# A state-space scan and a SwiGLU feed-forward on one core: smaller pieces of converted weights, and a last block that is stored in quarters and eighths

## The chip, the cores and the metric

The kernel runs on one core of a Trainium2 chip, in one launch. The metric is the device time of that core in microseconds. A core has TensorE (PE in the profile; PEld is its weight load), VectorE (DVE), ScalarE (ACT), GpSimd (POOL), SyncE (SP), which here issues nearly all DMAs, and 16 DMA engines.

## The reference

Two stages. The first is a Mamba-2 scan over x (4 batches, 8 heads, 768 tokens, 32 channels) with decays `a` and state matrices B and C (16 wide); its result, as 3072 tokens of 256 channels, is the input of the second, a gated feed-forward. Shortened:

```python
# scan, in chunks (the kernel takes 128 tokens as a chunk)
L = exp(cum[i] - cum[j]) * causal
y = ((C @ B.T) * L) @ x  +  (C @ state) * exp(cum)
state = exp(sum(la)) * state + sum_j B_j x_j * exp(cum[-1] - cum[j])
# feed-forward: x is (3072, 256), d_ff is 1536
xn = x / sqrt(mean(x * x) + 1e-6) * rms_g
g, val = xn @ w_gate, xn @ w_val
out = (g / (1 + exp(-g)) * val) @ w_out
```

w_gate, w_val and w_out come as 64-bit floating point, all else in 32 bits; the kernel makes 32-bit numbers of the weights on the chip.

## The kernel before

The 3072 tokens are worked on in six blocks of 512. While block n goes through the feed-forward, the scan makes the input of block n + 1, so that PE's products of both are interleaved. Blocks 1 to 5 take the products two by two in Strassen's way with seven products instead of eight (`product_gv`, steps P.k.j with k = 1 to 7 and j = 0 to 5 for 256 columns of d_ff; `product_o`, steps O.k.j). Sums of weights that these need are made by VectorE (`combine_w`, step cw; `combine_wo`, step two), sums of inputs too (`combine_x`, step tx; s, s2, s3, s4 for the hidden values). The partial results are taken out of PSUM by ScalarE (take), added by VectorE (C), go through SiLU on ScalarE (silu) and are multiplied on VectorE (hid). Block 0 takes the first columns with plain products (early.0, early.1, gate.2 to gate.5), the others in Strassen's way (there silu and hid are called silug and hidg), and its products with w_out are plain (o.0 to o.11).

The order of all this is written out by hand or by a planner: a string of steps for block 0, one for block 1, one for blocks 2 to 4 and one for block 5. The kernel runs through the string, and each engine executes its instructions in the order in which the steps issue them. A step that waits therefore holds up what comes after it on its engine.

Conversion of the weights is part of block 0. `fetch` issues the DMAs of a piece on SP's queue, as raw 32-bit words. `power(k)` (step pow) makes the power of two from the top 16 bits with three ScalarE instructions (lines 165, 166, 168), `mantissa(k)` (step man) makes the mantissa with two VectorE instructions (lines 175, 177), `weight(k)` (step wt) multiplies both (line 185) and issues the next fetch. Pieces before: two of 128 columns of both w_gate and w_val (512 elements a partition), five of 256 columns of both, three of w_out (1024 elements a partition each). The mantissa is made in the raw buffer itself; three large raw buffers exist.

Other steps that the prediction speaks of: spread fetches rows of sums of logarithms by a broadcast DMA, sub and ex (line 407) make decays of them, after which GpSimd masks them (line 408); load fetches B, C and x of a pair of chunks; rowout stores the sums of logarithms; turn, T, Tt, g, L, L1, A, S, y, sq, yt belong to the scan; ms, mc, mt, rs, rb, xn to the normalisation.

In block 5 the scan is over, and only the feed-forward runs. Its last product with w_out is k = 3, which adds onto product 5 in one PSUM bank, for two groups t of 128 tokens and 128 channels (a block is two groups t by two halves a of 128 tokens); `total_o` adds the taken partial results (Oadd, line 844) and `put_half` stores half a of the block's tokens, 256 KB, in one DMA (out, line 849).

Of the kernel before, what the change touches and what calls it, by code (L numbers as in the profile page):

```python
# [20 lines left out]
def kernel(  # L21
# [33 lines left out]
    nc = tc.nc  # L55
# [72 lines left out]
    pieces = [("gv", c, 128) for c in (0, 128)] + [("gv", c, 256) for c in range(256, DF, 256)]  # L128
    pieces += [("o", c, 4) for c in range(0, NF, 4)]
    fetched = []  # L130

    def fetch(k=1):
        for _ in range(min(k, len(pieces))):
            n, c, w = pieces.pop(0)
            if w == 128:
                r = ffn.tile([P, 8 * w], I32, tag="h", name="wr", bufs=NF // 2)
            else:
                r = raw.tile([P, 8 * 256], I32, tag="wr", name="wr", bufs=3)
            if n == "o":
                nc.sync.dma_start(out=r.rearrange("p (o m) -> p o m", o=w),  # L140
                                  in_=wsrc[n][:, c:c + w])
                dst = wo[:, c:c + w].rearrange("p o m -> p (o m)")
            else:
                both = r.rearrange("p (n t f) -> p n t f", n=2, t=2)
                for k, name in enumerate("gv"):
                    nc.sync.dma_start(out=both[:, k], in_=wsrc[name][:, :, 2 * c:2 * (c + w)])
                dst = wgv[:, :, :, c:c + w]
            w32 = r.rearrange("p (f w) -> p f w", w=2)
            fetched.append((r.bitcast(I16).rearrange("p (f w) -> p f w", w=4)[:, :, 3],
                            w32[:, :, 0], w32[:, :, 1], dst, w32.shape[1]))  # L150
# [10 lines left out]
    def power(k):  # L161
        words16, lo, hi, dst, n = fetched[k]
        e = cvt.tile([P, n], FP32, tag="e", name="e", bufs=2)
        k16, b16 = e.bitcast(I16)[:, n:2 * n], e.bitcast(I16)[:, 0:n]
        nc.scalar.activation(out=k16, in_=words16, func=AF.Relu, scale=1.0 / 16, bias=kinks[:, 0:1])  # L165
        nc.scalar.activation(out=e, in_=k16, func=AF.Prelu, scale=-1.0, bias=kinks[:, 1:2],  # L166
                             alpha=2.0 ** -20)
        nc.scalar.activation(out=b16, in_=e, func=AF.Prelu, scale=-2.0 ** 27, bias=kinks[:, 2:3],
                             alpha=2.0 ** -20)
        parts[k] = b16.bitcast(BF16)  # L170


    def mantissa(k):
        words16, lo, hi, dst, n = fetched[k]
        nc.vector.tensor_scalar(out=hi, in0=hi, scalar1=0xFFFFF, scalar2=0x100000,
                                op0=ALU.bitwise_and, op1=ALU.bitwise_or)
        nc.vector.scalar_tensor_tensor(out=lo.bitcast(FP32), in0=lo.bitcast(U32),
                                       scalar=2.0 ** -32, in1=hi, op0=ALU.mult, op1=ALU.add)

    def weight(k):  # L180
        words16, lo, hi, dst, n = fetched[k]
        f, e = lo.bitcast(FP32), parts.pop(k)
        if len(dst.shape) > 2:
            f, e = [v.rearrange("p (n t f) -> p n t f", n=2, t=2) for v in (f, e)]
        nc.vector.scalar_tensor_tensor(out=dst, in0=f, scalar=2.0 ** -20, in1=e,  # L185
                                       op0=ALU.mult, op1=ALU.mult)
        if k > 1:
            fetch()


    start = ffn.tile([P, 8, P], FP32, tag="ob", name="start", bufs=1)
    warm = start[:, 0].bitcast(BF16)
# [8 lines left out]
    fetch(1)  # L201
    gcol = const.tile([P, 2], FP32, name="gcol")
    nc.sync.dma_start(out=gcol, in_=moe_rms_g.rearrange("(t p) -> p t", p=P))
    fetch(2)
    load(2)
    load_x(2)
    fetch(2)
# [6 lines left out]
    ones = start[:, 5]  # L214
    nc.vector.memset(ones, 1.0)
    zeros = start[:, 1]
    nc.vector.memset(zeros, 0.0)
    upto = start[:, 2]
    nc.gpsimd.affine_select(out=upto, in_=ones, pattern=[[1, P]], compare_op=ALU.is_ge,
                            fill=0.0, base=0, channel_multiplier=-1)  # L220
    never = start[:, 3]
    nc.gpsimd.affine_select(out=never, in_=zeros, pattern=[[1, P]], compare_op=ALU.is_ge,
                            fill=-2.0 ** 100, base=0, channel_multiplier=-1)
    after = start[:, 4]
# [72 lines left out]
    mids = start[:, 6:8]  # L297
# [396 lines left out]
    spaces = []  # L694

    def piece_for_sums(k):
        while len(spaces) <= k // 2:
            spaces.append(raw.tile([P, 2, 8 * P], FP32, tag="wr", name="sums", bufs=3))
        return spaces[k // 2][:, k % 2]

    def combine_w(j):
        if j < NF // 4:
            s = piece_for_sums(j).rearrange("p (w k m) -> p w k m", w=2, k=4)
        else:
            s = const.tile([P, 2, 4, P], FP32, name="sw%d" % j)
# [39 lines left out]
    def taken_gv(blk, k, j):  # L745
        vs[k, j] = t = cvt.tile([P, 512], FP32, tag="p", name="p", bufs=4)
# [33 lines left out]
    def combine_wo(j0):  # L780
        js = slice(j0, j0 + 2)
        two[j0 // 2] = w = piece_for_sums(3 + j0 // 2).rearrange("p (k j m) -> p k j m", k=4, j=2)
# [29 lines left out]
    def product_o(blk, k, j):  # L812
        bank_of = {1: "X", 6: "X", 7: "X", 2: 2, 4: 4, 5: 5, 3: 5}[k]
        if k in (1, 2, 4, 5) and j == 0:
            val = k in (2, 5)
            Os[bank_of] = later[val].tile([P, 512], FP32, tag="val" if val else "gate",
                                          name="o", bufs=2)
# [7 lines left out]
        for t in range(2):  # L825
            nc.tensor.matmul(out=o[:, t * P:(t + 1) * P], lhsT=lhsT[:, t], rhs=rhs,  # L826
                             start=(k in (1, 2, 4, 5) and j == 0 and t == 0), stop=True,
                             skip_group_check=True)
# [11 lines left out]
    def total_o(blk, c):  # L840
        if blk not in obs:
            obs[blk] = ffn.tile([P, 2, 2, DM], FP32, tag="ob", name="ob", bufs=1)
        a, m, v, o = {11: (0, 0, 1, 2), 22: (1, 1, 7, 5), 21: (1, 0, 7, 4), 12: (0, 1, 6, 5)}[c]
        nc.vector.tensor_tensor(out=obs[blk][:, :, a, m * P:(m + 1) * P], in0=ts[v],
                                in1=halves_of(Os[o]), op=ALU.add)

    def put_half(blk, a):
        dst = out[blk * TB:(blk + 1) * TB, :].rearrange("(t a p) m -> p t a m", t=2, a=2)
        nc.sync.dma_start(out=dst[:, :, a], in_=obs[blk][:, :, a])

# [71 lines left out]
    def by_vector(out, in_, scale):  # L922
# [39 lines left out]
        mask.0.1 r.0 d parts.0 c turn.0.0 T.0.0 Tt.0.0.0 turn.0.1 sums.0.1 turn.1.0 T.0.1  # L962
        mask.0.0 Tt.0.0.1 Tt.0.1.0 dx sums.0.0 cx Tt.0.1.1 g.0.0 exp.0.1 T.1.0 turn.1.1 Tt.1.0.0
        scale.1 mask.1.1 exp.0.0 T.1.1 Tt.1.1.0 cc scale.0 L.0.0 Tt.1.0.1 sums.1.1 g.0.1
        Tt.1.1.1 A.0 g.1.1 exp.1.1 mask.1.0 pow.0 L.0.1 S.0 last.0 g.1.0 last.1 L.1.1 Tl.0
        sums.1.0 Tl.1 A.1 exp.1.0 y.0 man.0 r.1 sq.0 S.1 pow.1 L.1.0 wt.0 y.1 yt.0 ydone.0
        parts.1 scale.2 sq.1 early.0.0 pow.2 yt.1 man.1 mask.2.0 ms.0 mc.0 wt.1 sums.2.0 row.1
        ydone.1 early.0.1 mt.0 mask.2.1 rs.0 sums.2.1 turn.2.0 rowout.1 exp.2.0 mask.3.1 man.2
        exp.2.1 rb early.1.0 rc T.2.0 xn.0 Tt.2.0.0 norm.0 sums.3.1 early.1.1 wt.2 Tt.2.0.1
        pow.3 mask.3.0 exp.3.1 man.3 turn.2.1 row.0 T.2.1 Tt.2.1.0 sums.3.0 rowout.0 scale.3  # L970
        exp.3.0 Tt.2.1.1 pow.4 wt.3 gate.2 norm.1 gg.2 silu.0 pow.5 gate.3 load.4 A.2 man.4
        L.2.0 silu.3 L1.2.2 hid.0 wt.4 spread.8 S.2 silu.2 gate.4 hid.3 L1.2.3 switch.0 silu.1
        turn.3.1 hid.2 turn.3.0 T.3.0 silu.4 P.1.3 T.3.1 Tt.3.0.0 man.5 Tt.3.1.0 hid.4 take.1.3
        Tt.3.0.1 gate.5 table Tt.3.1.1 tx.0 silu.5 cw.3 wt.5 hid.5 cw.4 pow.6 y.2 P.1.4 A.3
        P.6.3 yt.2 take.6.3 gg.3 sq.2 S.3 man.6 P.7.3 take.1.4 L1.3.2 take.7.3 L.3.0 pow.7
        ydone.2 switch.1 L1.3.3 P.2.3 P.6.4 C.11.3 y.3 P.5.3 take.6.4 wt.6 P.4.3 tok man.7
        silug.21.3 P.2.4 yt.3 silug.11.3 hidg.21.3 P.7.4 sq.3 P.1.5 ms.1 C.22.3 hidg.11.3
        take.1.5 P.3.3 C.11.4 cw.5 wt.7 tokout take.7.4 C.12.3 P.5.4 silug.11.4 spread.9 ydone.3
        P.6.5 P.2.5 C.22.4 silug.22.3 silug.12.3 hidg.11.4 take.6.5 C.11.5 P.3.4 hid.1 mc.1
        pow.8 P.7.5 silug.22.4 sub.9 P.4.4 take.7.5 man.8 P.5.5 mt.1 hidg.12.3 hidg.22.3 wt.8  # L980
        o.0 rs.1 o.1 silug.21.4 o.2 C.22.5 spread.10 C.12.4 sub.8 o.3 P.3.5 pow.9 hidg.22.4
        silug.12.4 man.9 sub.10 spread.11 o.4 hidg.21.4 P.4.5 wt.9 scale.4 hidg.12.4 rb
        silug.22.5 C.12.5 ex.10 o.5 load.5 silug.11.5 sub.11 o.6 silug.21.5 xn.1 o.7 hidg.11.5
        hidg.22.5 ex.11 o.8 cw.0 o.9 ex.9 silug.12.5 hidg.21.5 hidg.12.5 o.10 cw.1 ex.8 tx.1
        o.11
# [19 lines left out]
    def of_chunk(n, fn):  # L1005
# [5 lines left out]
        "O": product_o, "Otake": taken_o, "Oadd": total_o, "out": put_half,  # L1011
        "cw": lambda blk, j: combine_w(j) if blk == 1 else None,
# [16 lines left out]
    for blk in range(1, NBLK):  # L1029
        if blk == 1:  # L1030
            order = """
                P.2.0 scale.1 P.1.1 P.1.0 P.2.1 take.1.1 turn.0.0 take.1.0 P.6.0 load.0 table
                C.11.1 P.5.1 take.6.0 P.6.1 take.6.1 P.7.0 silu.11.1 C.11.0 turn.0.1 silu.11.0
                take.7.0 T.0.0 P.7.1 P.5.0 two.0 take.7.1 P.4.0 Tt.0.0.0 C.22.1 hid.11.1
                silu.22.1 P.3.1 Tt.0.0.1 C.22.0 silu.21.0 T.0.1 silu.22.0 hid.21.0 P.4.1 P.1.2
                silu.21.1 hid.11.0 Tt.0.1.0 take.1.2 C.12.1 P.2.2 cw.2 P.3.0 spread.0 P.6.2
# [102 lines left out]
```

## Time and profile before

| | |
|---|---|
| median of 9 runs | 418.65 us (418.6 to 419.82) |
| the profiled execution | 418.61 us |
| its span, first to last instruction | 416.9 us |
| granted TensorE clock | 1.000 |
| PE busy | 410.2 us (98%), 3100 instructions |
| DVE busy | 309.1 us (74%), 635 instructions |
| ACT busy | 223.2 us (54%), 434 instructions |
| POOL busy | 41.3 us (10%), 48 instructions |
| DMA | 27.99 MB, 86516 packets |

Time outside the span (418.61 - 416.9 = 1.7 us) is that of the launch. Block 0 ends on PE at 99.0 us, block 1 at about 164.4, blocks 2 to 4 take about 64.6 us each and block 5 the last 55 us, up to the last matmul at 413.2 us. A timeline line gives start, duration (of the merged instructions from first to last), engine, line of the kernel, operation, what is written from what, shapes, how many, and in square brackets how long the engine was idle before and what ended that.

### The profile page before, as it was taken

The numbers are of one execution on the slowest core, as the hardware profiler recorded it, in microseconds if no ns is written. First come the engines' busy times: TensorE is split into PE (matmuls) and PEld (weight loads), VectorE is DVE, ScalarE is ACT, GpSimd is POOL, SyncE is SP. The second block draws the span as 40 slices with busy tenths as digits, with TensorE's granted clock in tenths as the row PEclk, the third lists the DMA queues.
The fourth block names the chain that finished last, engine by engine and source line by source line (L and its number), as shares of the span: only waits on it lengthen the run. The fifth ranks groups of instructions, "written<-read, shape, count | busy, mean of one in ns | idle before, by whom it ended". The sixth has DMA issues, their size and how long they took to land.

```text
span 416.9 us, 7846 instructions
## 1 busy us (share of the span) xinstructions
PE 410.2 (98%) x3100; PEld 343.9 (82%) x3100; DVE 309.1 (74%) x635; ACT 223.2 (54%) x434; POOL 41.3 (10%) x48
## 2 busy tenths in 40 slices
PE   8999999999999999999999999999999999999996
PEld 4675468888887899887899887889888889988996
DVE  6899899997767997566888567778667874555771
ACT  3789987987564434654418645326755421254410
POOL 3010010031000024000005100004200001000000
PEclk9999999999999999999999999999999999999999
DMA  9988846402303060505230503440100000100001
GB/s 111 228 241 209 195 152 254 49 1 61 42 2 103 22 131 0 102 2 89 63 102 20 83 2 68 85 102 2 51 2 1 2 2 0 52 1 2 0 2 50
DMA packets 86516, 27.99 MB, mean 67 GB/s; under 512 B 75952, under 2 KB 80304, under 8 KB 86480
## 3 DMA queue, kind: packets, MB, share of 16 engines
q1 hardware_dynamic: 82320, 27.24, 28.3%
q10 hardware_dynamic: 4160, 0.26, 0.7%
q8 instruction: 24, 0.39, 0.4%
q14 instruction: 12, 0.10, 0.1%
HBM read 24.22 MB, written 3.28 MB: 66 GB/s over the span
## 4 chain that ended last, share of the span: by engine, by line
PE 91%; ACT 4%; DVE 3%; issue 1%; DVEq 0%; ACTq 0%
PE gate L741 28%; PE o L826 23%; PE val L741 21%; PE o L773 5%; PE g L470 3%; PE y L552 2%; PE tp L436 2%; PE y L543 1%; PE gate L660 1%; PE A_ps L503 1%; PE e L365 1%; ACT e L166 1%; ACT e L165 1%; PE idle L268 1%; PE rb L615 1%
## 5 line engine op out<-in xcount | busy, mean ns | idle before, releaser
L753 DVE TENSOR_TENSOR c<-val,p 128x512 f32<-128x512 f32 x99 | 67.0, 687 | 42.1 <-PE val L741 32.2
L747 ACT COPY p<-gate 128x512 f32<-128x512 f32 x99 | 57.4, 585 | 64.4 <-PE gate L741 64.2
L766 DVE TENSOR_TENSOR h<-c 128x256 f32<-128x256 f32 x99 | 43.4, 459 | 11.6 <-ACT c L762 11.5
L762 ACT ACTIVATE c<-c 128x256 f32<-128x256 f32 x99 | 38.4, 416 | 13.5 <-DVE c L753 13.4
L741 PE MATMUL gate<-tx,sw 128*128 128x256 f32 x144 | 36.4, 382 | 0.0
L741 PE MATMUL gate<-xn,wgv 128*128 128x256 f32 x132 | 34.5, 389 | 0.7 <-DVE wgv L185 0.7
L838 ACT COPY v<-o 128x256 f32<-128x256 f32 x15 | 5.6, 372 | 53.3 <-PE o L826 53.3
L741 PE MATMUL val<-xn,wgv 128*128 128x256 f32 x132 | 33.9, 379 | 0.0
L741 PE MATMUL gate<-tx,wgv 128*128 128x256 f32 x132 | 33.8, 384 | 0.0
L826 PE MATMUL o<-wo,h 128*128 128x128 f32 x240 | 33.8, 275 | 0.0
L826 PE MATMUL o<-sums,h 128*128 128x128 f32 x240 | 32.7, 276 | 0.0
L571 POOL TENSOR_TENSOR sq<-sq 128x256 f32<-128x256 f32 x12 | 9.9, 824 | 225.3 <-ACT sq L570 194.9
L826 PE MATMUL o<-sums,s 128*128 128x128 f32 x240 | 31.8, 277 | 0.0
L741 PEld LDWEIGHTS gate<-tx,sw 128*128 128x128 f32 x144 | 27.0, 190 | 4.6 <-issue 0.7
L826 PEld LDWEIGHTS o<-wo,h 128*128 128x128 f32 x240 | 30.2, 192 | 0.2 <-issue 0.2
L826 PEld LDWEIGHTS o<-sums,h 128*128 128x128 f32 x240 | 29.6, 192 | 0.6 <-DVE h L766 0.5
L741 PE MATMUL gate<-tx,sums 128*128 128x256 f32 x120 | 30.0, 379 | 0.0
L826 PEld LDWEIGHTS o<-sums,s 128*128 128x128 f32 x240 | 29.1, 192 | 0.8 <-issue 0.8
L741 PEld LDWEIGHTS gate<-tx,wgv 128*128 128x128 f32 x132 | 24.6, 190 | 4.4 <-issue 1.0
L741 PEld LDWEIGHTS gate<-xn,wgv 128*128 128x128 f32 x132 | 23.5, 190 | 5.3 <-DVE h L766 1.5
L741 PEld LDWEIGHTS val<-xn,wgv 128*128 128x128 f32 x132 | 25.0, 190 | 3.4
L762 ACT ACTIVATE u<-gate 128x256 f32<-128x256 f32 x33 | 12.3, 381 | 24.3 <-PE gate L741 24.3
(165 smaller groups left out, 772.0 us busy)
## 6 DMA issues: line engine op xcount, KB each, us to landing
L<-rowd SPq DMA_DIRECT2D x16, 512.0 KB, 4.7
xr<-in_x_dram SPq DMA_DIRECT2D x24, 128.0 KB, 3.4
wr<-in_moe_w_out_dram SPq DMA_DIRECT2D x3, 1024.0 KB, 6.1
wr<-in_moe_w_gate_dram SPq DMA_DIRECT2D x5, 512.0 KB, 5.9
wr<-in_moe_w_val_dram SPq DMA_DIRECT2D x5, 512.0 KB, 6.8
out_dram<-ob SPq DMA_DIRECT2D x10, 256.0 KB, 2.2
br<-in_B_dram SPq DMA_DIRECT2D x22, 64.0 KB, 4.3
cr<-in_C_dram SPq DMA_DIRECT2D x22, 64.0 KB, 3.3
```

Of the source, the lines that this page charges most:

```text
L436: nc.tensor.transpose(out=tp[:, k], in_=src[:, i].rearrange("p h n -> p (h n)"), identity=ident)
L470: nc.tensor.matmul(out=g[:, 256 * i:256 * i + 256], lhsT=T[r, i, 0], rhs=T[r, i, 1:3].rearrange("p t m -> p (t m)"), start=(i == 0), stop= ...
L552: nc.tensor.matmul(out=y[o:o + 32, h // 4, i * P:(i + 1) * P], lhsT=s["x"][:, i, h], rhs=Ls[p][:, i, h], start=opens, stop=True, tile_posi ...
L571: nc.gpsimd.tensor_tensor(out=sqs[blk][:, tk], in0=sq2[:, 0], in1=sq2[:, 1], op=ALU.add)
L741: nc.tensor.matmul(out=dst[:, half[w]], lhsT=lhsT, rhs=rhs, start=(k in (1, 2, 5) and w == 0), stop=True, skip_group_check=True)
L747: nc.scalar.copy(out=t, in_=Xs[j])
L753: nc.vector.tensor_tensor(out=t, in0=Zs[j], in1=a, op=ALU.add)
L762: nc.scalar.activation(out=u, in_=src[:, half[0]], func=AF.Silu)
L766: nc.vector.tensor_tensor(out=hidden_tile(blk, j)[:, c // 10 - 1, c % 10 - 1], in0=u, in1=src[:, half[1]], op=ALU.mult)
L773: nc.tensor.matmul(out=o, lhsT=hs_[blk, f // 2][:, f % 2, k // 2, (k % 2) * P:(k % 2 + 1) * P], rhs=wo[:, f], start=opens, stop=(f == NF - ...
L826: nc.tensor.matmul(out=o[:, t * P:(t + 1) * P], lhsT=lhsT[:, t], rhs=rhs, start=(k in (1, 2, 4, 5) and j == 0 and t == 0), stop=True, skip ...
L838: nc.scalar.copy(out=ts[k], in_=halves_of(Os["X"]))
```

## The change

Three things change together.

- The weights are converted in pieces of half the size, each of one matrix: for w_gate and w_val two pieces each of 128 columns (256 elements a partition) and five each of 256 columns (512), for w_out six of two rows of tiles (512). So pow, man and wt number 0 to 19 instead of 0 to 9. The raw buffers are six of half the size (and four small ones); the mantissa is written to a tile of its own (`m`), so a raw buffer is free after pow and man. wt issues a fetch each time. The tiles of `taken_gv` share four buffers with the powers' (`e`). The first constants no longer share a tile with the output.
- In block 5 the last product's bank is split: product 5 and product 3 of each 128 tokens t accumulate in two banks of their own. The last product runs for t = 0, then for t = 1 (`products_of_t`, step Ot); Oadd.12 is made for each t apart; of half a = 0 the first 128 channels are stored for both t at once (128 KB, quarter.0.0), the other 128 channels for each t apart (64 KB, quarter.0.1.0 and quarter.0.1.1). Half a = 1 is stored as before.
- All four orders are new.

```diff
+    wdst = {"g": wg, "v": wv, "o": wo}
+    pieces = [(n, c, w) for c, w in [(0, 128), (128, 128)] + [(c, 256) for c in range(256, DF, 256)]
+              for n in "gv"]
+    pieces += [("o", c, 2) for c in range(0, NF, 2)]
...
+            small = shape[0] * shape[1] == 256
+            r = raw.tile([P, shape[0], 2 * shape[1]], I32, tag="ws" if small else "wr",
+                         name="wr", bufs=4 if small else 6)
+            nc.sync.dma_start(out=r, in_=src)
...
     def mantissa(k):
-        words16, lo, hi, dst, n = fetched[k]
-        nc.vector.tensor_scalar(out=hi, in0=hi, scalar1=0xFFFFF, scalar2=0x100000,
+        words16, (lo, hi), dst, shape = fetched[k]
+        m = cvt.tile(shape, I32, tag="m", name="m")
+        nc.vector.tensor_scalar(out=m, in0=hi, scalar1=0xFFFFF, scalar2=0x100000,
                                 op0=ALU.bitwise_and, op1=ALU.bitwise_or)
-        nc.vector.scalar_tensor_tensor(out=lo.bitcast(FP32), in0=lo.bitcast(U32),
-                                       scalar=2.0 ** -32, in1=hi, op0=ALU.mult, op1=ALU.add)
+        parts[k, "f"] = f = m.bitcast(FP32)
+        nc.vector.scalar_tensor_tensor(out=f, in0=lo.bitcast(U32), scalar=2.0 ** -32, in1=m,
+                                       op0=ALU.mult, op1=ALU.add)
...
-        if k > 1:
-            fetch()
+        fetch()
...
-    fetch(1)
+    fetch(2)
     gcol = ...
-    fetch(2)
+    fetch(4)
     load(2)
     load_x(2)
-    fetch(2)
+    fetch(3)
     load(3)
     load_x(3)
...
-    def product_o(blk, k, j):
+    def product_o(blk, k, j, ts=(0, 1)):
...
+        apart = bank_of == 5 and blk == NBLK - 1
+            if apart:
+                Os[5] = [bank("o", (P, P)) for t in ts]
...
+        for t in ts:
+            nc.tensor.matmul(out=o[t] if apart else o[:, t * P:(t + 1) * P], lhsT=lhsT[:, t],
+                             rhs=rhs, start=(k in (1, 2, 4, 5) and j == 0 and (apart or t == 0)),
+                             stop=True, skip_group_check=True)
+
+    def products_of_t(blk, k, t):
+        for j in range(NF // 2):
+            product_o(blk, k, j, (t,))
...
+    def put_quarter(blk, a, m, t=None):
+        dst = out[blk * TB:(blk + 1) * TB, :].rearrange("(t a p) m -> p t a m", t=2, a=2)
+        t, ms = slice(0, 2) if t is None else slice(t, t + 1), slice(m * P, (m + 1) * P)
+        nc.sync.dma_start(out=dst[:, t, a, ms], in_=obs[blk][:, t, a, ms])
```

The order of block 0 before and after, from the first plain products on (the part before that is the scan's first two pairs and the first four conversions; after, it begins with load.4):

```
before
        parts.1 scale.2 sq.1 early.0.0 pow.2 yt.1 man.1 mask.2.0 ms.0 mc.0 wt.1 sums.2.0 row.1
...
        exp.3.0 Tt.2.1.1 pow.4 wt.3 gate.2 norm.1 gg.2 silu.0 pow.5 gate.3 load.4 A.2 man.4
        L.2.0 silu.3 L1.2.2 hid.0 wt.4 spread.8 S.2 silu.2 gate.4 hid.3 L1.2.3 switch.0 silu.1
        turn.3.1 hid.2 turn.3.0 T.3.0 silu.4 P.1.3 T.3.1 Tt.3.0.0 man.5 Tt.3.1.0 hid.4 take.1.3
        Tt.3.0.1 gate.5 table Tt.3.1.1 tx.0 silu.5 cw.3 wt.5 hid.5 cw.4 pow.6 y.2 P.1.4 A.3
...
        o.0 rs.1 o.1 silug.21.4 o.2 C.22.5 spread.10 C.12.4 sub.8 o.3 P.3.5 pow.9 hidg.22.4
        silug.12.4 man.9 sub.10 spread.11 o.4 hidg.21.4 P.4.5 wt.9 scale.4 hidg.12.4 rb
        silug.22.5 C.12.5 ex.10 o.5 load.5 silug.11.5 sub.11 o.6 silug.21.5 xn.1 o.7 hidg.11.5
        hidg.22.5 ex.11 o.8 cw.0 o.9 ex.9 silug.12.5 hidg.21.5 hidg.12.5 o.10 cw.1 ex.8 tx.1
        o.11
after
        yt.0 wt.1 sq.1 ydone.0 early.0.0 man.2 rowout.1 pow.4 parts.1 scale.2 ms.0 yt.1 mask.2.0
...
        sums.3.0 norm.0 T.2.1 tx.0 exp.3.0 Tt.2.1.0 Tt.2.1.1 silu.0 scale.3 norm.1 rowout.0
        gate.2 pow.7 wt.6 man.7 gg.2 silu.2 hid.0 man.8 L.2.0 hid.2 gate.3 L1.2.2 spread.8 wt.7
        turn.3.0 gate.4 pow.8 silu.3 L1.2.3 wt.8 pow.9 man.9 T.3.0 spread.9 hid.3 Tt.3.0.0
        silu.1 A.2 Tt.3.0.1 wt.9 switch.0 man.10 gate.5 turn.3.1 pow.10 man.11 silu.4 cw.3 wt.10
        pow.11 hid.4 P.1.3 S.2 silu.5 T.3.1 take.1.3 spread.10 y.2 Tt.3.1.0 wt.11 A.3 hid.5
        Tt.3.1.1 man.12 P.1.4 man.13 pow.12 gg.3 S.3 P.6.3 yt.2 sq.2 ydone.2 switch.1 P.2.3
...
        hidg.12.4 hidg.11.5 silug.21.5 wt.18 wt.19 sub.8 xn.1 P.3.5 C.12.5 silug.22.5 cw.0 ex.9
        sub.10 o.6 o.7 silug.12.5 hidg.12.5 o.8 hidg.22.5 ex.10 ex.11 o.9 hidg.21.5 ex.8 tx.1
        o.10 o.11 cw.1
```

The end of block 5's order:

```
before
        O.7.5 Otake.7 O.4.4 O.4.5 s4.2 s4.0 O.2.5 Oadd.22 O.3.0 Oadd.11 O.3.1 O.3.2
        O.3.3 O.3.4 Oadd.21 out.1 O.3.5 Oadd.12 out.0
after
        O.6.0 s2.5 O.6.1 O.6.2 s2.4 O.6.3 s3.3 s3.5 O.6.4 O.6.5 s3.4 Otake.6 O.2.3 s4.3
        O.4.3 O.7.0 O.7.1 O.7.2 O.4.4 O.7.3 s4.0 O.7.4 s4.5 s4.1 s4.2 O.7.5 Otake.7
        Oadd.22 O.2.4 O.2.5 O.4.5 s4.4 Oadd.11 Oadd.21 quarter.0.0 out.1 Ot.3.0
        Oadd.12.0 Ot.3.1 quarter.0.1.0 Oadd.12.1 quarter.0.1.1
```

## The prediction

> **What bounds the kernel now.** I read the page's 40 slices first, then the table by windows, then the timeline of the conversions, of the end of block 0 and of the last microseconds.
>
> ```profile
> PE   8999999999999999999999999999999999999996
> DVE  6899899997767997566888567778667874555771
> ACT  3789987987564434654418645326755421254410
> ```
>
> A slice is 10.4 us. TensorE (PE) is full everywhere but at the two ends. VectorE (DVE) and ScalarE (ACT) are nearly full only in the first ten slices, which is block 0 with the conversion of the weights. The windows (columns: PE, PEld, DVE, ACT, POOL busy, clock, DMA) put numbers on it:
>
> ```profile
> 22.00:42.00 20.00, 19.78 (x133) 12.40 (x131) 18.95 (x32) 18.24 (x24) 1.77 (x2) 1.00 0.85 231
> 42.00:58.00 16.00, 15.33 (x112) 8.08 (x110) 13.95 (x28) 14.56 (x22) 0.00 (x0) 1.00 0.65 161
> 58.00:81.00 23.00, 22.91 (x155) 18.87 (x155) 22.38 (x35) 19.04 (x31) 3.16 (x3) 1.00 0.61 178
> 81.00:99.00 18.00, 18.00 (x88) 15.83 (x87) 17.86 (x30) 13.23 (x14) 4.67 (x4) 1.00 0.00 1
> ```
>
> From 22 to 99 us VectorE idles 1.05 + 2.05 + 0.62 + 0.14 = 3.9 us, ScalarE 1.8 + 1.4 + 4.0 + 4.8 = 11.9 us, of which 7.2 us lie before 81. Three engines run almost without a gap, and PE waits only where another is late. The clearest place is P.1.4:
>
> ```profile
> 55.61 1.13 PE L741 MATMUL gate<-xn,wgv 128*128 128x256 f32 x4 [0.67 <-DVE wgv L185]
> ```
>
> After 58 us PE runs without a wait to the last product at 413.18 us; VectorE idles 15 us or more in each of blocks 1 to 4. So time can change in two places: before about 100 us, where PE can be starved, and behind the last product.
>
> **The change part by part.** The sum is made against the profiled execution: 418.61 us, of which the span is 416.9; the median of nine runs is 418.65. About 0.2%, 0.84 us, is what a measurement of this kernel can tell from no change.
>
> *Conversion in smaller pieces.* Before: 2 pieces of 512 elements a partition and 8 of 1024. After: 4 of 256 and 16 of 512. Ten pieces more, each with three ScalarE and three VectorE instructions.
>
> ```profile
> 13.95 0.76 ACT L165 ACTIVATE e<-wr,kinks 128x512 int16<-128x512 int16 x1
> 14.73 0.72 ACT L166 ACTIVATE e<-e,kinks 128x512 f32<-128x512 int16 x1
> ...
> 25.79 0.41 DVE L175 TENSOR_SCALAR wr<-wr 128x512 int32<-128x512 int32 x1
> 26.24 0.70 DVE L177 SCALAR_TENSOR_TENSOR wr<-wr 128x512 f32<-128x512 uint32 x1
> 26.98 0.69 DVE L185 SCALAR_TENSOR_TENSOR wgv<-wr,e 128x512 f32<-128x512 f32 x1
> ...
> 31.34 1.23 ACT L165 ACTIVATE e<-wr,kinks 128x1024 int16<-128x1024 int16 x1
> 32.61 1.15 ACT L166 ACTIVATE e<-e,kinks 128x1024 f32<-128x1024 int16 x1
> ...
> 34.17 0.69 DVE L175 TENSOR_SCALAR wr<-wr 128x1024 int32<-128x1024 int32 x1
> 34.90 1.23 DVE L177 SCALAR_TENSOR_TENSOR wr<-wr 128x1024 f32<-128x1024 uint32 x1
> 36.91 1.22 DVE L185 SCALAR_TENSOR_TENSOR wgv<-wr,e 128x1024 f32<-128x1024 f32 x1
> ```
>
> VectorE: 0.41 + 0.70 + 0.69 = 1.80 us a small piece, 0.69 + 1.23 + 1.22 = 3.14 a large one, so two small cost 0.46 more. ScalarE (its third step costs what the second does): 2.20 against 3.53, so 0.87 more. The 256 pieces aren't in the trace; the straight line through both sizes gives the same surcharge. Ten times: VectorE +4.6 us, ScalarE +8.7 us. Mantissas in a tile of their own have the same shapes; the rows read and write with a stride already, so I take no difference (bounds: 0.3 us of 4.6 either way).
>
> *What of it reaches PE.* The last products of block 0, o.10 and o.11, need hidg.12.5 and its neighbours, and before they come just in time:
>
> ```profile
> 90.85 2.32 POOL L408 TENSOR_SCALAR_AFFINE_SELECT L<-L 128x1024 f32<-128x1024 f32 x2 [3.84 <-ACT L L407]
> 90.93 2.51 DVE L766 TENSOR_TENSOR h<-c 128x256 f32<-128x256 f32 x2
> 95.16 0.42 DVE L766 TENSOR_TENSOR h<-c 128x256 f32<-128x256 f32 x1
> ```
>
> hidg.12.5 ends at 95.58; the second half of o.10, which needs it, is issued at about 96.4 (o.11 follows at 97.26). VectorE has 0.8 us to spare there and 4.6 us of new work ahead. One thing pays back: two L766 beside GpSimd's masks take 2.51 us instead of 0.84, about 0.87 for each mask. The masks come with the ex steps; the old order has ex.10, ex.11 and ex.9 ahead of hidg.12.5, the new one only ex.9: two stalls fewer, -1.75. VectorE would then be ready at 95.58 + 4.6 - 1.75 = 98.4 less what it regains of its 3.7 us of gaps before 81: a delay of 2.0 us with none regained, nothing from 2.0 us up.
>
> ScalarE is tighter. Of its 8.7 us, 2.6 belong to w_out, whose last piece before is ready at 86.0 for use at 92.1: covered by 6 us. The other 7 x 0.87 = 6.1 us belong to w_gate and w_val and lie before about 70 us, against 7.2 us of gaps, among them waits for PE and VectorE that don't simply go. All gaps used: no delay. None: 6.1 us. The steps behind them (take, silu) release PE's banks, so what is left is PE's. I take 60% regained, since the order is made anew and half-size pieces fit into gaps better: 6.1 - 4.3 = +1.8 us. VectorE's 2.0 is then covered by the same delay, not added to it.
>
> The new order also switches ScalarE's function table less after 81 us: before, ex and silug alternate and six loads of 1.28 us stand in the trace (81.32, 85.70, 87.70, 91.75, 93.48, 95.84); in the new order ex.9, silug.12.5, then the other three ex: four loads, 2.6 us less. They lie in the window where ScalarE idles 4.8 us, so I count nothing. The Trainium skill, "ScalarE: Activation LUTs", section "Rules for kernel authors", budgets about 2.7 us for a switch; this trace has 1.28. By the page the two would be 5.4 us, and still nothing in the sum.
>
> *DMAs and queues.* The bytes are the same. Weight matrices come one by one, and load.4 is moved to the head of block 0, so on SP's queue it is past all later fetches. The piece of w_val for columns 768 on, landed at 30.8 before, comes behind loads 3 and 4: load 3's landings follow it by 4.5 us, as much again for load 4 gives about 39 to 40. Its pow.9 stands between gate.4 and gate.5, after 44.5 before: hidden by 4 us, and whatever it exceeds that would be a wait of ScalarE. A fetch now waits for the man and pow that free one of six raw buffers; rowout and spread.8 stand behind it on SP, and spread.8 ran at 54.63 before, late enough. Nothing counted. In blocks 1 to 4 PE was full and VectorE had gaps; another order there is worth 0, between -0.5 and +0.5.
>
> *The end.* After the last product, before:
>
> ```profile
> 413.21 0.42 DVE L844 TENSOR_TENSOR ob<-v,o 128x256 f32<-128x256 f32 x1 [1.93 <-PE o L826]
> ...
> DMA to landing us min/median/max: 2.1/2.2/2.6
> ...
> DMA to landing us min/median/max: 1.7/1.8/2.3
> ```
>
> The landings are those of the 256 KB stores (L849; the last took 2.16) and of block 0's 128 KB stores (L854). After, the same 24 matrix instructions run as two dozens, and the first token half is added and stored under the second. Behind the last matmul stay one add of 128x128 from PSUM (0.28 in the row of L515: -0.14) and a store of 64 KB. Halving saved about 0.4 (2.2 to 1.8); halving again in proportion 0.2: landing about 1.6, -0.58. Together -0.7. Bounds: no better than the slowest 128 KB store (2.3, worth +0.14 against 2.16), then 0.0; 0.4 for each halving, then -0.9. The earlier stores are issued 1 to 2.5 us sooner and are out of the way. Oadd.22, now two adds, must precede the last product in its banks; O.2.4, O.2.5 and O.4.5 (1.3 us of PE) cover it. The two banks are free, as block 5 turns nothing. The Trainium skill, "DMA: Bandwidth & Descriptors", section "Rules for kernel authors", speaks against such stores: under 64 KB one pays mostly overhead, many small ones should be one. By a fixed cost alone the end would gain only the 0.14 of the add, and the sum would be 420.3; the two sizes in the trace say that size does count.
>
> Sum: 418.61 + 1.8 - 0.7 = 419.7 us.
>
> **Rivals.** *Faster.* tx.0, 1.4 us on VectorE, stands right ahead of the wait at 55.61 before, and some 100 steps earlier in the new order. If smaller pieces fill every gap, P.1.4's wait of 0.93 us (start to start) goes, and nothing comes in its place: 418.61 - 0.9 - 0.7 = 417.0; half of it, 417.5. For it: work ahead of P.1.4 is less by tx.0. Against it: P.1.4 now waits for two pieces (wt.10, wt.11), pow.11 being 2.2 us of ScalarE close before. It decides where ScalarE regains over 6 of its 7.2 us.
>
> *No difference.* ScalarE regains some 5.4 us, the start loses 0.7 and the end gives it back: 418.6.
>
> *ScalarE as the bound of block 0.* Only a quarter of the gaps is regained: 6.1 - 1.8 = 4.3, less 0.7: 422.2. For it: 8.7 us of new work against 7.2 us of gaps up to 81. Against it: w_out's pieces can slip.
>
> *The small store gains nothing:* 0.6 more on any of these; 2 in 10, and within the chances below.
>
> **How the numbers follow.** Slower by over 0.2% needs a start that loses over 1.5 us: 47 in 100 (my case, 419.7, with 37, and ScalarE as the bound, 422.2, with 10). Within 0.2%, the case of no difference: 28. Faster, by the rival of that name: 25. The range from 417.2 to 421.9 leaves out 1 in 10 at each side: below, the wait at 55.61 gone entirely; above, ScalarE as the bound. The slower case alone: 419.5 to 422.2.
>
> **What would show it.** Right: block 0's o.11 starts at 98.5 to 99.5 instead of 97.26; ScalarE idles under 4 us between 22 and 81; PE waits for it or for VectorE appear between 45 and 90 us; blocks 1 to 4 stay within 0.5 us; from the last matmul to the last landing 1.9 to 2.1 us instead of 2.6. Wrong: o.11 at 97.3 or sooner (the gaps did take all of it); a last landing no sooner; a block 1 to 4 that is longer or shorter by over 0.5 us.

## The result, and the profile after

The changed kernel takes 417.42 us in the median of 13 runs (416.7 to 417.71), the kernel before 418.67 in the 40 runs beside it; the ratio is 0.9957 [0.9948, 0.9966], so 1.4 to 2.2 us faster. I had forecast 419.7: the sign was wrong, though 417.42 lies within the range. Executions of both kernels fall in two groups, by whether the first products on PE are drawn out, at up to 1.67 times their time (last section): their medians are 418.61 and 419.80 us before, 416.96 and 417.43 after, a gain of 1.65 us in one group and of 2.37 in the other. The ratio is that of the means; the medians of all runs are only 1.25 us apart.

The changed kernel's profiled execution takes 417.43 us, its span 415.71. The profile of before begins without the drawn-out first products, that of after with them. Stage by stage on PE:

| | before | after | difference |
|---|---|---|---|
| block 1 begins (block 0 is done) | 98.98 | 99.21 | +0.23 |
| blocks 1 to 4 | 259.00 | 258.58 | -0.42 |
| block 5, to the last matmul | 55.18 | 55.18 | 0 |
| last matmul to last landing | 2.65 | 1.89 | -0.76 |
| last landing to the end of the span | 1.07 | 0.84 | -0.24 |

Block 0 is shorter too, when like is set beside like. Without drawn-out first products it ends at 98.98 before and at 98.77 with the changed block 0 (in run e10 below): -0.21. With them it ends at 100.17 with the old block 0 (in run e12) and at 99.21 with the new one: -0.96. What the first products shift can be left out: from the start of early.0.0 to the end of block 0 PE takes 76.9 us with the old block 0 (before, e2, e12) and 76.0 with the new one (after, e3, e10, e11), 0.9 less. The experiments on block 0 below are compared by this stretch.

The page's slices of the changed kernel, which answer to those of before:

```profile
PE   8999999999999999999999999999999999999997
DVE  5899998979679986376986477795575784556672
ACT  2998998877646316745428645526646431245410
```

ScalarE's second and third slices (10.4 to 31.2 us) are 9 and 9 where 7 and 8 stood: its work begins sooner. The windows, with the same stretches as before:

```profile
22.00:42.00 20.00, 20.00 (x167) 12.69 (x161) 19.59 (x45) 17.73 (x29) 2.27 (x3) 1.00 0.91 189
42.00:58.00 16.00, 16.00 (x123) 8.25 (x123) 15.52 (x32) 15.65 (x29) 0.00 (x0) 1.00 0.67 177
58.00:81.00 23.00, 23.00 (x151) 18.90 (x144) 21.36 (x42) 19.58 (x36) 1.46 (x2) 1.00 0.62 210
81.00:99.00 18.00, 18.00 (x88) 15.68 (x87) 15.38 (x29) 14.54 (x21) 4.41 (x4) 1.00 0.00 1
```

PE's first number equals the length in every row: from 22 to 99 us the profile shows no wait of it, where it lost 0.22 + 0.67 + 0.09 = 0.98 us before. ScalarE idles 2.27 + 0.35 + 3.42 = 6.0 us up to 81, against 7.2. P.1.4 starts without the bracket that named the wait:

```profile
55.93 1.13 PE L732 MATMUL gate<-xn,wgv 128*128 128x256 f32 x4
```

At the end, a shorter add stands behind the last matmul, and the table of the last stores (in the DMA view from 405 us on) gives the landings by size:

```profile
413.01 0.29 DVE L846 TENSOR_TENSOR ob<-v,o 128x128 f32<-128x128 f32 x1 [1.05 <-PE o L822]
...
out_dram<-ob SPq DMA_DIRECT2D x1, 256.0 KB, 2.2
out_dram<-ob SPq DMA_DIRECT2D x1, 128.0 KB, 1.9
out_dram<-ob SPq DMA_DIRECT2D x2, 64.0 KB, 1.5
```

### The profile page after: what moved, and what is told of

It is laid out like the page before. It is cut to its first block, busy times and chain, and to the rows that moved or that the text cites. A ratio compares the mean times of both kernels' runs of the same rounds, so it can differ in the third digit from the quotient of the medians.

```text
span 415.7 us, 7936 instructions
## 1 busy us (share of the span) xinstructions
PE 411.9 (99%) x3100; PEld 345.0 (83%) x3100; DVE 304.5 (73%) x667; ACT 229.4 (55%) x462; POOL 39.0 (9%) x48
## 3 DMA queue, kind: packets, MB, share of 16 engines
HBM read 24.22 MB, written 3.28 MB: 66 GB/s over the span
## 4 chain that ended last, share of the span: by engine, by line
PE 99%; DVE 0%; issue 0%
PE gate L732 28%; PE o L822 23%; PE val L732 21%; PE o L764 5%; PE g L468 4%; PE gate L648 3%; PE y L550 3%; PE tp L434 2%; PE y L541 2%; PE gate L658 2%; PE e L363 1%; PE A_ps L501 1%; PE rb L613 1%; PE e L374 1%; PE idle L266 1%; PE ms L591 1%
## 5 line engine op out<-in xcount | busy, mean ns | idle before, releaser
L732 PE MATMUL gate<-tx,sw 128*128 128x256 f32 x264 | 65.0, 382 | 0.0
L732 PEld LDWEIGHTS gate<-tx,sw 128*128 128x128 f32 x264 | 48.7, 190 | 8.2 <-issue 2.0
L732 PE MATMUL val<-xn,sw 128*128 128x256 f32 x132 | 34.1, 383 | 0.0
L732 PE MATMUL val<-tx,sw 128*128 128x256 f32 x132 | 33.8, 384 | 0.0
L822 PE MATMUL o<-two,s 128*128 128x128 f32 x240 | 32.0, 275 | 0.0
L569 POOL TENSOR_TENSOR sq<-sq 128x256 f32<-128x256 f32 x12 | 10.1, 842 | 226.9 <-ACT sq L568 196.9
L822 PE MATMUL o<-two,h 128*128 128x128 f32 x240 | 30.9, 275 | 0.0
L822 PEld LDWEIGHTS o<-two,s 128*128 128x128 f32 x240 | 29.9, 192 | 0.3
L822 PEld LDWEIGHTS o<-two,h 128*128 128x128 f32 x240 | 28.9, 192 | 0.1
L732 PEld LDWEIGHTS val<-tx,sw 128*128 128x128 f32 x132 | 24.5, 190 | 4.6 <-DVE h L757 1.0
L732 PEld LDWEIGHTS val<-xn,sw 128*128 128x128 f32 x132 | 24.4, 190 | 4.2 <-issue 0.7
```

Of the source, the lines that this page charges most:

```text
L569: nc.gpsimd.tensor_tensor(out=sqs[blk][:, tk], in0=sq2[:, 0], in1=sq2[:, 1], op=ALU.add)
L732: nc.tensor.matmul(out=dst[:, half[w]], lhsT=lhsT, rhs=rhs, start=(k in (1, 2, 5) and w == 0), stop=True, skip_group_check=True)
L822: nc.tensor.matmul(out=o[t] if apart else o[:, t * P:(t + 1) * P], lhsT=lhsT[:, t], rhs=rhs, start=(k in (1, 2, 4, 5) and j == 0 and (apar ...
```

## The experiments

**The parts alone.** e2 has the old kernel with block 5's new end, e3 the changed kernel with the old end (Ot and quarter put back to O.3.0 to O.3.5 and out.0).

```diff
 e2, the last lines of block 5's order
-    O.2.5 Oadd.22 O.3.0 Oadd.11 O.3.1 O.3.2 O.3.3 O.3.4 Oadd.21 out.1 O.3.5 Oadd.12 out.0
+    O.2.5 Oadd.22 Oadd.11 Oadd.21 quarter.0.0 out.1 Ot.3.0 Oadd.12.0 Ot.3.1
+    quarter.0.1.0 Oadd.12.1 quarter.0.1.1
```

> The kernel before with the change of block 5's end alone: product 3 apart in two banks, quarters and eighths. Prediction's term: -0.7. From the two traces: the way from the last matmul to the last landing shrinks by 0.75 us, and the waits behind the landing by 0 to 0.25, according to which of the eight DMA semaphores the last store gets (here the sixth one in turn, second of five waits: -0.06). Expected 417.8 to 417.95. If the small store gains nothing: 418.5.

> The changed kernel with the old end in block 5 (one bank, one half stored at the end). If the parts add up: 417.4 + 0.75 + about 0.1 for the waits behind the last landing = 418.2 to 418.4, so that small pieces and new orders together are worth -0.2 to -0.5 instead of the +1.8 that the prediction gave them. Rival (the tail gained more in the changed kernel than the traces show): 418.7 or above.

e2: 418.35 us, ratio 0.9982 [0.997, 0.9995]; from the last matmul to the last landing 1.90 us instead of 2.65. e3: 417.85, ratio 0.9971 [0.996, 0.9982], with 2.63 us there. The end is worth 0.73 to 0.76 us in either kernel, and what is left of the gain comes with the new orders and pieces.

e12 has the old block 0, pieces and order, with all else changed.

> The kernel before in all of block 0 (large pieces, its order) and the changed kernel's orders of blocks 1 to 5 and its end. From the traces: blocks 1 to 4 -0.44, the end -0.75, the waits behind it -0.06 to -0.2: about 417.3 where the kernel before has 418.65. If this is above the changed kernel's 417.4 in the same runs, the new block 0 is worth something of its own; if it is below, the new block 0 costs something.

417.28 us, ratio 0.996 [0.9947, 0.9973]: by these two numbers not to be told from the changed kernel. By its profile blocks 1 to 4 take 65.06, 64.40, 64.34 and 64.67 us, the changed kernel 65.16, 64.40, 64.34 and 64.67: their gain is that of their own orders. Block 0 takes 76.89 us from early.0.0 on, the changed kernel 75.97; the new block 0 with its smaller pieces brings no more than the 0.2 to 1.0 us named above.

**What smaller pieces cost where nothing is moved.** e1 is the kernel before, with each conversion instruction cut into two halves; e5 cuts ScalarE's alone, e6 VectorE's alone.

```diff
+        for h in (slice(0, n // 2), slice(n // 2, n)):
-        nc.scalar.activation(out=k16, in_=words16, func=AF.Relu, ...)
+            nc.scalar.activation(out=k16[:, h], in_=words16[:, h], func=AF.Relu, ...)
 (so too the two other steps of power, those of mantissa and that of weight)
```

> The kernel before, with its orders, its DMAs and its large raw buffers, but every conversion instruction cut in two: the same extra 30 ScalarE and 30 VectorE instructions (8.7 and 4.0 to 4.6 us) as in the changed kernel, and nothing else. Theory 'the new order hides it' (the surcharge is real; the changed order pays it out of places that the old one does not use: ScalarE before 22 us, exponentials and sums put behind the last hidden values): block 0 ends 2 to 4 us later than 98.98, 420.7 to 422.7 us. Rival 'slack' (what ScalarE and VectorE do later was never needed by PE): block 0 ends within 0.5 us of 98.98, 418.5 to 419.2 us. The prediction's own pricing (60% of the gaps regained) says +1.8, or more since the masks stay where they were.

> The kernel before with only ScalarE's conversion instructions cut in two (+8.7 us on ScalarE, none on VectorE). Cutting both made the old order 3.4 to 3.8 us longer. Theory 'ScalarE is what PE waits for' (as the prediction had it): 421 to 422.4 us with this alone. Rival 'VectorE': under 419.4. Both together: about 420.5.

> The kernel before with only VectorE's conversion instructions cut in two (+4.0 to 4.6 us on VectorE, none on ScalarE). Theory 'ScalarE is what PE waits for': 418.6 to 419.4 us. Rival 'VectorE': 421 to 422.4. Both together: about 420.5.

e1: 422.5 us, ratio 1.0078 [1.0061, 1.0095]. e5: 421.25, 1.0053 [1.0034, 1.0072]. e6: 419.97, 1.003 [1.0016, 1.0043]. From early.0.0 on block 0 takes 80.18 us in e1's profile, 78.97 and 78.18 in e5's and e6's, against 76.90: +3.28, +2.07 and +1.28. The two engines' shares add up (3.35); neither covers the other. What was added is 8.6 us of ScalarE, as in the change, and 5.2 of VectorE, more than the change's 4.0. PE's waits between 10 and 115 us in e1 (waits, total us, times, longest):

```profile
PE y L562 <- DVE L L490: 1.1, 1, 1.1
PE tp L446 <- DVE L L501: 0.9, 1, 0.9
PE gate L660 <- ACT L L398: 0.7, 1, 0.7
PE gate L751 <- DVE wgv L195: 0.4, 1, 0.4
```

Most lie in the scan's steps; the conversion itself is waited for only in the last line, P.1.4's.

e13 asks the same of the new order: every other piece of the changed kernel (ten of twenty) is cut in two.

```diff
+    def cuts_of(k):
+        return (0, 1) if k % 2 == 0 else (slice(0, 2),)
...
+        for h in cuts_of(k):
+            nc.scalar.activation(out=k16[:, h], in_=words16[:, h], func=AF.Relu, ...)
```

> The changed kernel, in which every other piece's conversion instructions (ten pieces of twenty, three on ScalarE and three on VectorE each) are cut in two, nothing moved: about the surcharge of the change once more, some 4 us of VectorE and 8 us of ScalarE. Theory (the new order gives PE work that doesn't wait for the conversion where VectorE and ScalarE are late, so block 0 has room): under half of the old order's 3.2 us, so 417.4 to 418.9. Rival (each instruction more costs what it costs in the old order, and the new order merely begins from a better place): +3.2, 420.6, with PE waits between 25 and 95 us. Third possibility: the new order is at its limit and loses more than the old one, over 421.

421.05 us, ratio 1.0038 [1.0023, 1.0054]; block 0 takes 79.75 us from early.0.0 on against 75.99, +3.76, for 8.6 us more of ScalarE and 4.5 of VectorE. My theory of room in the new order falls: a surcharge of this size costs 3 to 4 us in either order. Between the rival (the same cost) and the third possibility (more than in the old order, over 421) this doesn't decide. The sums over 10 to 99 us, of before, of the changed kernel and of e13 in turn:

```profile
sum 89.00, PE 88.02 PEld 62.80 DVE 83.36 ACT 74.86 POOL 10.33; mean PE 17.60 PEld 12.56 DVE 16.67 ACT 14.97 POOL 2.07
```
```profile
sum 89.00, PE 89.00 PEld 62.91 DVE 81.80 ACT 78.86 POOL 8.48; mean PE 17.80 PEld 12.58 DVE 16.36 ACT 15.77 POOL 1.70
```
```profile
sum 89.00, PE 86.79 PEld 59.90 DVE 80.97 ACT 80.26 POOL 7.00; mean PE 17.36 PEld 11.98 DVE 16.19 ACT 16.05 POOL 1.40
```

The changed kernel is full on PE. VectorE and ScalarE still idle 7.2 and 10.1 of the 89 us, but e13's additions didn't go into these gaps without holding up PE. So the change paid for its own surcharge, and the question is with what.

**What pays for it.** Each run takes one thing back in the changed kernel; so it shows what the new order loses without this thing, not what the old order would gain with it. e7 puts o.0, o.1 and o.2 (5.2 us of PE's work that needs no weight still in conversion) just ahead of o.3:

```diff
-        silug.22.3 P.7.4 o.0 table silug.21.3 take.7.4 pow.15 o.1 mc.1 ... silug.21.4 P.1.5 o.2 wt.16
+        silug.22.3 P.7.4 table silug.21.3 take.7.4 pow.15 mc.1 ... silug.21.4 P.1.5 wt.16
-        silug.22.4 P.6.5 pow.17 scale.4 hidg.11.4 o.3
+        silug.22.4 P.6.5 pow.17 scale.4 hidg.11.4 o.0 o.1 o.2 o.3
```

> The changed kernel with o.0, o.1 and o.2 (5.2 us of PE) moved in the order to just ahead of o.3, so behind P.4.4, P.2.5, P.3.4, P.1.5 and P.6.5; nothing else is moved. Theory 'early o products cover the slower conversion' (the new order gives PE work at 70 us that needs no late weights, and the old order has none): PE waits for take.7.4, cw.5 or wt.13 in their place, block 0 ends 1 to 4 us later than 99.2, 418.5 to 421.5 us. Rival (the place of the o's doesn't matter, the steps before 22 us do): 417.2 to 417.8 us.

421.99 us, ratio 1.0089 [1.0057, 1.012]; block 0 takes 80.32 us from early.0.0 on, 4.35 more, most of the cover. PE now waits for what VectorE and ScalarE take from PSUM:

```profile
PE val L732 <- DVE c L744: 2.0, 1, 2.0
PE gate L732 <- ACT p L738: 1.8, 2, 1.1
```

e14 puts tx.0 back behind gate.5.

```diff
-        sums.3.0 norm.0 T.2.1 tx.0 exp.3.0
+        sums.3.0 norm.0 T.2.1 exp.3.0
-        gate.5 turn.3.1
+        gate.5 tx.0 turn.3.1
```

> The changed kernel with tx.0 (1.4 us of VectorE) put back behind gate.5, ahead of P.1.4, where it stood before. The prediction's rival of the faster side (P.1.4's wait went because tx.0 left its place): a wait of PE at P.1.4 comes back, 0.7 to 0.9 us, 418.2 in the median. Theory (P.1.4 is covered by more than that: the smaller pieces and what stands behind it): no wait at P.1.4, block 0 longer by under 0.3 us, 417.4.

418.58 us, ratio 0.9983 [0.9971, 0.9995]; block 0 takes 77.15 us from early.0.0 on, 1.18 more, most of tx.0's 1.4. The wait returned, though a step earlier than the rival said, at y.2, which waits for a hid (this reads its product from PSUM):

```profile
PE y L541 <- DVE h L681: 1.0, 1, 1.0
```

e15 puts ex.10 and ex.11 ahead of silug.12.5 and hidg.12.5.

```diff
-        sub.10 o.6 o.7 silug.12.5 hidg.12.5 o.8 hidg.22.5 ex.10 ex.11 o.9
+        sub.10 ex.10 ex.11 o.6 o.7 silug.12.5 hidg.12.5 o.8 hidg.22.5 o.9
```

> The changed kernel with ex.10 and ex.11 (and so two of GpSimd's masks) put back ahead of silug.12.5 and hidg.12.5, as in the old order. The prediction's term (two stalls of VectorE beside masks fewer, 1.75 us, and less of ScalarE ahead): hidg.12.5 ends 1.7 to 4 us later than 96.46, PE waits for it at o.8 to o.10, block 0 ends at 100.2 to 102 instead of 99.2, 418.5 to 420. Rival (there is room ahead of o.10): hidg.12.5 later, but no wait of PE, 417.4.

422.36 us, ratio 1.0072 [1.0053, 1.0091]; block 0 takes 81.40 us from early.0.0 on, 5.4 more. ScalarE, then VectorE, then PE:

```profile
95.39 2.00 ACT L405 ACTIVATE L<-L 128x1024 f32<-128x1024 f32 x2 [4.95 <-DVE L L399]
97.41 1.28 ACT L753 ACT_TABLE_LOAD   x1
98.71 0.42 ACT L753 ACTIVATE c<-c 128x256 f32<-128x256 f32 x1
```
```profile
99.16 0.76 DVE L757 TENSOR_TENSOR h<-c 128x256 f32<-128x256 f32 x2 [3.79 <-ACT c L753]
```
```profile
99.64 4.42 PE L764 MATMUL o<-wo,h 128*128 128x256 f32 x12 [3.65 <-DVE h L757]
```

hidg.12.5 comes at 99.16 instead of 96.04, and PE waits 3.65 us for it in the middle of o.10, whose second half and o.11 are the 12 products left. The other 1.8 us are lost behind the wait, where the granted clock is 0.50 for a while (last section). hidg.12.5 is late through ScalarE: two ex and a table load (3.28 us) stand ahead of silug.12.5, not stalls of VectorE. Part of the loss is the experiment's own, since sub.10 stands later in the new order than in the old and ex.10 waits for it (until 95.39); so it bounds what moving ex is worth from above.

e9 makes the mantissa in the raw buffer again (`m = hi`, the result in `lo`), with each pow ahead of its man, as this needs.

> The changed kernel with the mantissas made in the raw buffer again, as before, and so with each pow put ahead of its man where the order had them the other way round (the power must read the words first); pieces, other orders and the new end stay. A man now waits for ScalarE's first step of its piece, and a raw buffer is held up to the product. Theory 'the tile of its own matters' (VectorE runs ahead of ScalarE in block 0, fetches come sooner): 418.5 to 422 us. Rival 'only the order of PE's work matters': 417.0 to 417.8.

429.73 us, ratio 1.0249 [1.0229, 1.0268]; block 0 takes 89.94 us from early.0.0 on against 75.99, +13.9. VectorE waits for ScalarE's reading of the same words:

```profile
DVE wr L177 <- ACT e L167: 13.4, 9, 3.9
```

PE's own waits add up to 8.0 us, and for 10.2 us (38.9 to 42.3 and 66.2 to 73.0) its granted clock is 0.50, which by halving the pace could cost 5.1 more (an estimate). So the 13.9 is that of the whole experiment: the coupling, the steps that had to change places, the raw buffers held longer, and the clock that the waits brought down.

e4 and e8 were to show the large pieces in the new order. e4 takes the new order's man ahead of pow as it stands, so that powers are made from words that the mantissa has masked already, which changes that part of the computation; e8 has each pow first, and load.5 later.

> The kernel before (large pieces, mantissas in place, old end) with all of the changed kernel's orders, each large piece's steps where the small pair's were. Theory 'the new order hides it' (VectorE and ScalarE bound block 0 in the new order too, and PE runs out of waits only just): with 8.7 and 4.0 us less work block 0 ends no later than 99.2, and at best 0.5 to 1.5 us sooner than 98.98: 417.2 to 418.4. Rival 'the pieces help by their size' (results of half a piece come sooner, so that large pieces in this order make PE wait): block 0 ends 0.5 to 2 us later than 99.2: 418.9 to 420.4.

> The kernel before (large pieces, mantissas in place, three raw buffers, old end) with all of the changed kernel's orders; each large piece's power and mantissa stand where the first step of the small pair stood, the power first, the product where the second small one stood (w_out: the first); load.5 is moved behind wt.13, since SP would else hold the next weights behind it. To be compared with the changed kernel's pieces under the same orders and the old end: 417.85. Theory 'in the new order too the surcharge is what decides': block 0 ends up to 1 us sooner, 417.0 to 417.8. Rival 'half the size is what the new order lives on' (first halves sooner, a raw buffer free without the product, six instead of three): PE waits for weights, 419 to 423 us.

439.4 us (1.0484) and 447.43 (1.0683). In e4 VectorE waits 13.1 us for a piece of w_val, in e8 29.7 us for ScalarE's reading; in both the clock falls to 0.50 in between, as in e9. Both tell of buffers, as e9 does, and nothing on the size of a piece. Large pieces with a mantissa tile of their own weren't tried, so what half the size is worth by itself in the new order stays open.

**The end.** e11 stores the last two 64 KB as one 128 KB behind both adds; e10 cuts three stores of blocks 3 and 4 in two.

```diff
 e11
-    Ot.3.1 quarter.0.1.0 Oadd.12.1 quarter.0.1.1
+    Ot.3.1 Oadd.12.1 quarter.0.1
 e10, put_half
+        if (blk, a) in ((3, 0), (3, 1), (4, 0)):
+            for t in range(2):
+                nc.sync.dma_start(out=dst[:, t, a], in_=obs[blk][:, t, a])
+            return
```

> The changed kernel with its last two 64 KB stores as one of 128 KB, behind the second add; the product stays apart in two banks. Prediction's term: 0.2 us for the last halving. From the last matmul to the last landing: 2.05 to 2.15 us instead of 1.9; plus 0.05 to 0.1 by another semaphore. Rival 'size doesn't count, only the add does': 1.9. Time 417.2 to 417.8, within noise of the changed kernel's.

> The changed kernel with three of the eight stores of blocks 3 and 4 cut in two, far from the end of the span: only the count of DMAs changes, so that the last store gets the semaphore that the closing waits ask for first instead of last. If that is where 0.24 us behind the last landing came from, the stretch from the last landing to the end of the span is 1.0 us again instead of 0.8. Rival (it came from the size of the last store): 0.8.

e11: 417.75 us, 0.9962 [0.9946, 0.9977]; 2.17 us from the last matmul to the last landing, where the changed kernel has 1.89. The second halving is worth 0.28, of its 0.76. e10 (one execution, 417.23): the landing is unchanged at 1.92, and the span ends 1.07 us behind it, as in the kernel before, not 0.84. SP waits at the end for the DMA semaphores in a fixed order, two at a time, 0.06 us each. The last store of before has number 104, which is in the first wait; the changed kernel's has 109, in the last; three DMAs more bring 104 again. The other runs stand in between: 1.03 us with 106 (e2), 0.97 with 107 (e3), 0.90 with 108 (e11). The 0.24 us of the last row of the table is this turn of numbers, and no merit of the stores.

## Why the prediction was right or wrong

**The end held.** -0.7 was forecast, -0.76 came; the 64 KB store landed in 1.54 us (1.6 forecast), the add took 0.29 (0.28). Size did count, 2.2, 1.9 and 1.5 us for 256, 128 and 64 KB, though a quarter of the size still takes two thirds of the time. The Trainium skill's "DMA: Bandwidth & Descriptors", section "Rules for kernel authors", puts transfers under 64 KB down as mostly overhead; none was run here.

**Blocks 1 to 4** gave -0.42, inside the bound of 0.5 and near its end: -0.07, -0.24, -0.19 and +0.08. Why blocks 2 and 3 are shorter is left open.

**The surcharge was sized rightly**: VectorE's conversions rose by 4.0 us (4.6 forecast), ScalarE's by 8.8 (8.7 forecast; its whole busy time by 6.2, as two table loads of 1.28 are gone). That 60% of ScalarE's gaps would take it up, so that 1.8 us reach PE, is near what e5 measures where nothing is moved: 2.07.

**The step that failed is "What of it reaches PE".** It priced the surcharge in the old order's gaps and charged that to the new order. In place of its +1.8, block 0 came out 0.9 us shorter from early.0.0 on, although the same surcharge costs some 3 us where nothing is moved. Two things in it were wrong:
- "VectorE's 2.0 is then covered by the same delay, not added to it": e6 has 1.28 of its own, and e1 with both has 3.28. The price in the old order was not 1.8.
- It set nothing on the other side but two stalls and some gaps. The new order moves other work out from ahead of the places where PE is served just in time. tx.0 was seen and set at nothing except in a rival: putting it back costs 1.18 of its 1.4 us (e14). The ex steps were priced as two stalls of VectorE; e15 shows them to stand on ScalarE's way to hidg.12.5, where they cost PE a wait of 3.65 us. The early o.0 to o.2 weren't priced: 4.35 of their 5.2 us (e7). For the mantissa's own tile only the instructions were priced, at "no difference", and not the order that it permits: with mantissas in place the new order loses 13.9 us (e9). These overlap and can't be added. That together they pay for the surcharge and for PE's old waits follows by elimination; no run puts them into the old order, so the share of each isn't shown. e13 shows that the new order has no room left for as much again.

What came out at PE is then simple: its waits from 10 to 99 us went from 0.98 to 0.00. That is the 0.9 us from early.0.0 on. With drawn-out first products early.0.0 starts as before (23.24, 23.28 in e12), and the gain stays whole; without them it starts 0.69 us later (22.78 in e10, 22.09), and 0.21 is left. ScalarE is busier from 10 to 22 us in both (11.36 and 11.06 of 12 us, 9.79 before), since a part of the surcharge lies there; whether that is why early.0.0 comes later isn't shown.

**The rival of the faster side** had the place right, the wait of 0.93 us at P.1.4 gone with nothing after it, and its 417.0 is near. Its condition was wrong: ScalarE didn't regain over 6 of its 7.2 us, its gaps shrank to 6.0 only; of its 8.8 us of surcharge 1.3 (e10 against before) to 2.2 (after against e12) went ahead of 22 us and 3.6 behind 81, where it had no conversion before, and other work of ScalarE left the stretch between. That the wait went because the smaller pieces fill the gaps isn't shown either: e14 brings a wait back by moving tx.0 alone. Of the signs I had named, o.11 at 98.5 to 99.5 (97.48 came), ScalarE's idle time under 4 us (6.0) and PE waits between 45 and 90 (none) failed; the 1.9 to 2.1 us at the end (1.89) and blocks 1 to 4 held. **The closing**, 0.24, wasn't foreseen.

## What to carry to other kernels

Where three engines run just in time, 13 to 14 us of work added on the two engines that serve PE cost 3.3 to 3.8 us here, while single pieces put back in a tight place cost most of their length (4.35 of 5.2, 1.18 of 1.4). So when a change adds work and rewrites an order by hand or planner, list what stands ahead of each tight place before and after, engine by engine, and price both lists, not the old order's gaps. A buffer that two engines change in place couples them as firmly as a data dependency does: ask, before calling a copy of its own free of effect, which orders it permits. A wait can cost more than its length: one of 3.65 us brought the clock down and cost 1.8 us more (e15), one of 2.0 us didn't (e7). At the end of a kernel, cutting the last product and its store pays down to 64 KB here.

## What the runs showed of the hardware

Two executions of the same first instructions, of before and of e12 (whose block 0 is the same), on PE:

```profile
5.51 0.67 PE L306 MATMUL r_ps<-start,la 128*128 128x256 f32 x2
6.01 0.81 PE L330 MATMUL d_ps<-la,start 128*128 128x192 f32 x4
```
```profile
5.51 1.19 PE L306 MATMUL r_ps<-start,la 128*128 128x256 f32 x2
6.49 1.49 PE L330 MATMUL d_ps<-la,start 128*128 128x192 f32 x4
```

Single matmuls take 634 ns instead of 379 and 527 instead of 326, 1.67 and 1.62 times as long, until about 10 us. The windows show a granted clock of 1.00 there in both, but without a record: the traces' first clock records, of 1.00, stand at 5.12 us in before, at 10.00 in e12 and at 9.46 in the changed kernel, where the slow products end. A clock of 0.50 is on record in e15, for 3.41 us behind the wait of 3.65:

```profile
99.70:102.80 3.10, 3.10 (x8) 2.47 (x9) 3.07 (x7) 3.06 (x3) 1.10 (x1) 0.50 0.02 5
```

There products of 128x256 take 634 ns again, and they start 427 ns apart instead of 216, which is a ratio of 2. So the slow beginning is most likely the same halved clock (argued from these durations; no record covers it). The shift stays to the end: early.0.0 starts at 23.28 instead of 22.09, 1.19 us, and that is the distance between the two medians of the kernel before. The Trainium skill's "TensorE: Matmul & The Clock Gate" (section "Part 1: The HAM clock gate") describes a clock that is halved until a free-running window has seen PE busy, so that the number of slow products differs from run to run. The halving agrees with e15's 0.50; what decides the length of the slow beginning no run here tests. With the new order the two starts lie only 0.46 us apart (22.78 and 23.24); I take it that less of block 0's beginning hangs on those products, as the sums of pair 0 come sooner and d later, but no run shows it apart.

VectorE's additions of two tiles in SBUF take 0.42 us, but 1.19 to 1.30 us while GpSimd masks; after the change the masks meet tx.1, which PE doesn't wait for (its trace has no wait up to 164 us):

```profile
97.28 2.36 POOL L406 TENSOR_SCALAR_AFFINE_SELECT L<-L 128x1024 f32<-128x1024 f32 x2 [4.72 <-ACT L L405]
97.50 1.19 DVE L709 TENSOR_TENSOR tx<-xn,tx 128x256 f32<-128x256 f32 x1
98.61 1.30 DVE L709 TENSOR_TENSOR tx<-xn 128x256 f32<-128x256 f32 x1
```
